# Where a segment's output rows are stored from: GpSimd at its end, or SP inside the next segment

## The chip, the cores and the metric

One Trainium2 chip, one NeuronCore of it. The metric is the device time of one execution in microseconds. Engines: TensorE (PE, its weight loads PEld), VectorE (DVE), ScalarE (ACT), GpSimd (POOL) and SyncE (SP), each with a queue of its own that it works through in order. SP and GpSimd issue DMAs here; all transfers run on the same 16 DMA engines.

## The reference

Two independent parts, whose results stand side by side in the output's columns. Part A is a dilated sliding-window attention over 2048 rows. Part B, in which the change lies, is a recurrence over 64 segments of 32 rows. Each segment puts 8 memory rows in front of its own 32, runs an attention with 32 heads of 192 over these 40 rows, and its first 8 output rows are the memory of the next segment:

```python
for s in range(n_seg):
    xs = x[:, s * seg_len:(s + 1) * seg_len, :].copy()
    h = jnp.concatenate([mem, xs], axis=1)
    q = jnp.einsum('btd,dhe->bhte', h, Wq)
    k = jnp.einsum('btd,dhe->bhte', h, Wk)
    v = jnp.einsum('btd,dhe->bhte', h, Wv)
    scores = jnp.einsum('bhqe,bhke->bhqk', q, k) * scale
    ...
    p = _softmax(scores, axis=-1)
    o = jnp.einsum('bhqk,bhke->bhqe', p, v)
    o = jnp.einsum('bhte,hed->btd', o, Wo)
    mem = o[:, :M, :].copy()
    outs.append(o[:, M:, :])
```

Here `Dm` is 640, `M` is 8 and `seg_len` is 32. The weights of part B are bfloat16, 640 x 6144 each for q, k and v and 6144 x 640 for the output, more than fits on the chip beside the rest.

## The kernel before

**Tiling.** The 32 heads go in 4 groups of 8. Of each weight matrix a group has pieces: five for q, k and v (one per 128 rows of the input, 128 x 1536, 384 KB) and six for the output (128 x 1280, 320 KB). Most pieces stay in SBUF (`wres`). The 23 of `STREAMED` do not fit: they are copied once to DRAM in a layout that reads well (`wcopy`), and each segment fetches them again: k0 has 3 streamed pieces, k1 2, k2 3, v0 1, k3 2, v1 2, the output's group 0 one (o3), v2 2, v3 3, and the output four more (o15, o16, o20, o21). "k2" is the key projection of group 2.

**Time order.** The rows of a segment are split: the memory and the first 24 rows of the segment are its `main` 32 columns; the last 8 rows of several segments are projected together ahead of time (`ahead`), and their q and k are kept in blocks (`Lb`, made by line 591, `turn_late`) until the segment that uses them, which copies them into place (line 607, `fill_late`). Every segment renews one group of k and one of v (`RENEW`: k0 and v2 in each fourth segment, and so on); then its projection works on `ahead` and `main` together, and the `ahead` half goes first to the one buffer `sb` (line 567).

**Order of the work.** `ORDER` lists the steps of a segment by name, and the program is written in that order; TensorE, VectorE, ScalarE and SP keep it, while GpSimd's order is made by a scheduler. `q`, `k`, `v` with a group are projections (line 561), `e` and `ve` empty their PSUM banks (lines 567, 600, 614, 616), `T` turns the result and fills the late columns, `S` is the scores (line 625), `sb` to `send` the softmax, `tp` and `PT` spread it, `mix` multiplies by v (line 688), `ot` keeps the result (line 696) and sends its late rows from GpSimd to DRAM (lines 697 and 698, `late_o`), `out` and `last` are the output projection (lines 713 and 739), and `close` ends the segment: it writes the next segment's memory into `HX` (line 747), the segment's 32 rows into the tile `XS` (line 748), and stores 24 of them with four DMAs from GpSimd (line 750), one for each 160 columns.

**The fetches.** A step that needs a streamed piece asks `get_unit`, which issues the fetch of it from SP (line 474) into one of seven slots (`nbuf` 7) at that place of the program. SP runs ahead of TensorE: it issues a fetch as soon as the slot's former piece is used up, that is seven fetches ahead. SP also loads the next segment's rows into `XS` (line 534, `load_x`, at step `ve.2`), after the stores have read it.

**What the change touches.** `close` (lines 743 to 751) and `step` inside `segment` (lines 766 to 831), and by them the order of SP's and GpSimd's queues around the end of a segment. Behind the stores, GpSimd has at that place the block copies of the next q group (line 591, step `Tql`) and the fill of the next segment's q0 (line 607, step `T.q0`).

Of the kernel before, what the change touches and what calls it, by code (L numbers as in the profile page):

```python
# [23 lines left out]
def part_a(ctx, tc, A_x, A_wqkv, A_wo, out, ident, emit_loads):  # L24
# [241 lines left out]
    with tc.manual_schedule(engines={mybir.EngineType.PE, mybir.EngineType.DVE, mybir.EngineType.Activation}):  # L266
        pq = ps_q.tile([128, BIG], FP32, tag="q")
        for _ in range(LEAD_IN):
            nc.tensor.matmul(pq[:, 0:8], lhsT=ident, rhs=ident[:, 0:8], start=True, stop=True)
# [35 lines left out]
EVACUATE = {"k0": "SV", "k1": "SS", "k2": "VS", "k3": "VS", "q0": "VV", "q1": "SS", "q2": "VS", "q3": "VS"}  # L305
HEADS = ("SV", "SV", "SS", "SV")
SPREAD = "SSVV"
LEAD_IN = 114
HEAD = 10

# [8 lines left out]
def part_b(ctx, tc, B_x, B_mem0, B_Wq, B_Wk, B_Wv, B_Wo, out, ident, n_seg, pre, nbuf, mid):  # L319
    nc = tc.nc  # L320
    Dm, H, Dh, M, SEG, L = 640, 32, 192, 8, 32, 40
# [3 lines left out]
    out2 = out.rearrange("b s d -> (b s) d")  # L325
# [203 lines left out]
    def turn32(dst, src):  # L529
        nc.vector.transpose(dst, src.rearrange("p (f k) -> p k f", k=5))  # L530
# [39 lines left out]
    def turn_in_place(t):  # L570
        nc.vector.transpose(t, t)  # L571

    def columns_of(m, n0, n1):
        t = KT[:] if m == "k" else QT[:, 0:12 * L].rearrange("p (f n) -> p f n", n=L)
        return t[:, :, n0:n1]
# [19 lines left out]
    def project_qk(s, m, g):  # L595
        return project32([ahead, main] if renewed(s, m, g) else [main], m, g)

    def evacuate(m, ps, copies):
        sb = to_sb(ps[0], copies[0]) if len(ps) > 1 else None
        copies[1](columns_of(m, 0, 32), ps[-1][:].rearrange("p (f n) -> p f n", n=32))  # L600
        return sb

    def fill_late(s, m, g, sb):
        if sb is not None:
            return turn_late(sb, m, g, s, s)
        b = late.pop((m, g, s))
        nc.gpsimd.tensor_copy(columns_of(m, 32, L), b[:])  # L607
        free.append(b)

    def values(s, g):  # L610
        return project32([ahead, main] if renewed(s, "v", g) else [main], "v", g)

    def keep_values(g, ps):
        S_(Vst[:], ps[-1][:])  # L614
        if len(ps) > 1:
            S_(LV[g][:], ps[0][:])

    def scores(g):
        Sps = bank()[:, 0:4 * L].rearrange("p (a n) -> p a n", n=L)
        for outer in range(2):  # L620
            for a in range(4):
                for h in range(2):
                    k0, k1, c = (0, 128, 2 * h) if outer else (64 * h, 64 * h + 64, 1)
                    f = 3 * a + c
                    nc.tensor.matmul(Sps[64 * h:64 * h + 64, a, :], lhsT=QT[k0:k1, L * f:L * f + 64], rhs=KT[k0:k1, f, :],  # L625
                                     start=(outer == 0 and a == 0), stop=(outer == 1 and a == 3),
                                     tile_position=(k0, 64 * h))
        return Sps

    def soft_begin(Sps):  # L630
        nc.vector.scalar_tensor_tensor(out=Sps, in0=Sps, scalar=scale,  # L631
                                       in1=mask[:].unsqueeze(1).to_broadcast([128, 4, L]),
                                       op0=ALU.mult, op1=ALU.add)
        return Sps

    def soft_max(t1):
        mx = small.tile([128, 4], FP32, tag="mx")
        nc.vector.tensor_reduce(out=mx[:], in_=t1[:], axis=AX.X, op=ALU.max)
        return mx

    def soft_exp(t1, mx):
        nc.vector.tensor_tensor(t1[:], t1[:], mx[:].unsqueeze(2).to_broadcast([128, 4, L]), op=ALU.subtract)  # L642
        nc.scalar.activation(t1[:], t1[:], ACTF.Exp)  # L643

    def soft_end(s, g, t1):
        sm = small.tile([128, 4], FP32, tag="mx")
        nc.vector.tensor_reduce(out=sm[:], in_=t1[:], axis=AX.X, op=ALU.add)
        nc.vector.reciprocal(sm[:], sm[:])
        put_p(s, g, t1, sm)
# [18 lines left out]
    def spread_p(g, pt):  # L668
        PT = one.tile([128, 4, 2, L], BF16, tag="PT")
        if SPREAD[g] == "S":  # L670
            for b in range(2):
# [71 lines left out]
    def close(s, Y, part, partT):  # L743
        Ysb, T = XS[:], Vst[:, 0:320].bitcast(FP32).rearrange("p (k n) -> p k n", n=SEG)
        if s + 1 < n_seg:
            turn32(T, Y)
            nc.vector.tensor_tensor(HX[:, 0, :, 0:M], T[:, :, 0:M], partT[:, :, 0:M], op=ALU.add)
        nc.vector.tensor_tensor(Ysb, Y, part, op=ALU.add)  # L748
        for j in range(4):
            nc.gpsimd.dma_start(out2[SEG * s:SEG * s + SEG - M, Dm + 160 * j:Dm + 160 * j + 160],  # L750
                                Ysb[32 * j + M:32 * j + SEG])

    def segment(s):
        last = s + 1 == n_seg
        engine = {"S": S_, "V": V_}
        got = {}

        def project(m, g):
            if m == "v":
                got["v", g] = values(s, g)  # L760
            else:
                got[m, g] = project_qk(s, m, g)
                if last and (m, g) == ("k", 3):
                    load_late((2, 3))

        def step(name, *at):
            g = int(at[0][-1]) if at else None
            if name in "qkv":
                project(name, g)
            elif name == "e":  # L770
                m = at[0][0]
                got["sb", m, g] = evacuate(m, got.pop((m, g)), [engine[c] for c in EVACUATE[at[0]]])
            elif name == "T":
                m = at[0][0]
                keep = fill_late(s, m, g, got.pop(("sb", m, g)))
                turn_in_place(columns_of(m, 0, 32))
                if m + at[0][1] == "k0" and s and keep:
                    got["keep"] = keep
                elif keep:
                    keep()  # L780
                if at[0] == "k1" and "keep" in got:
                    got.pop("keep")()
            elif name == "S":
                got["S", g] = scores(g)
            elif name == "sb":
                got["t", g] = soft_begin(got.pop(("S", g)))
            elif name == "mx":
                got["mx", g] = soft_max(got["t", g])
            elif name == "sub":
                soft_exp(got["t", g], got.pop(("mx", g)))  # L790
            elif name == "send":
                soft_end(s, g, got.pop(("t", g)))
            elif name == "tp":
                got["p", g] = turn_p(g)
            elif name == "PT":
                got["PT", g] = spread_p(g, got.pop(("p", g)))
            elif name == "ve":
                keep_values(g, got.pop(("v", g)))
                if g == 2:
                    load_x(s + 1)  # L800
                elif last and g == 1:
                    load_late((0, 1))
            elif name == "mix":
                got["mix", g] = mix(g, got.pop(("PT", g)))
            elif name == "ot":
                keep_mix(s, g, got.pop(("mix", g)), [engine[c] for c in HEADS[g]])
            elif name == "out":
                g, half = int(at[0]), int(at[1])
                if "Y" not in got:
                    got["Y"] = ps_y.tile([128, 320], FP32, tag="y", name="Y")  # L810
                project_out(got["Y"], g, range(4 * half, 4 + 2 * half))
            elif name == "part":
                got["part"] = join_begin(got["Y"])
            elif name == "join":
                join_end(got["Y"], got["part"])
                got["partT"] = None if last else turn_part(got["part"])
            elif name == "tx":
                turn_x(s + 1)
            elif name == "ql":
                got["ql"] = None if last else project32([ahead], "q", (s + 1) % 4)  # L820
            elif name == "eql":
                got["sbl"] = None if last else to_sb(got["ql"][0], S_)
            elif name == "last":
                got["Z"] = bank()[:, 0:160]
                project_last(got["Z"])
            elif name == "close":
                close(s, got["Z"], got["part"], got["partT"])
            elif name == "Tql":
                if not last:
                    gl = (s + 1) % 4  # L830
                    turn_late(got["sbl"], "q", gl, s, s + 1)()

        for token in (ORDER if s else FIRST).split():
            step(*token.split("."))
# [3 lines left out]
    def load_late(quads):  # L838
        for b in quads:
            nc.sync.dma_start(res[DEAD[b]], late_o[b].rearrange("p g i c -> p (g i c)"))  # L840
# [143 lines left out]
```

## Time and profile before

| what | value |
|---|---|
| median of 3 runs | 1889.4 us (1887.69 to 1894.31) |
| the profiled execution | 1890.7 us |
| its span, first to last instruction | 1888.9 us |
| first and last stores of a segment | 211.4 to 1824.4 us |
| SP's waits for a slot (line 474, on the projections) | 744.3 us |
| four stores on GpSimd | 2.02 us |

Part A fills the first 200 us or so, the 64 segments run from there to about 1824 us, and a projection of all late rows ends the kernel. A row of the timeline gives start, duration, engine, line, operation, what is written and read, the count, and in brackets the idle time of the engine before it with what ended it. A row of the waits gives who waited for whom, the total in us, the number of times and the longest. In the windows the columns are the stretch, its length, the busy time of PE, PEld, DVE, ACT and POOL with their instructions, the granted TensorE clock, the busy share of the DMA engines and GB/s.

### The profile page before, as it was taken

How to read it: one execution, taken by the hardware profiler on the slowest of the kernel's cores; microseconds unless marked ns; L12 is line 12 of the kernel's file. 1: busy time of each engine (PE TensorE's matmuls, PEld its weight loads, DVE VectorE, ACT ScalarE, POOL GpSimd, SP SyncE). 2: the span in 40 equal slices, each digit the busy share in tenths (PEclk: the TensorE clock that was granted, in tenths of full speed). 3: DMA queues.
4: the chain of work that ended last, by engine and by line, in shares of the span. 5: the costliest groups of instructions: out<-in, count | busy, mean ns of one | idle time of the engine just before them, and what ended most of it. 6: DMA issues, size and time to landing. Idle time of an engine off the chain costs nothing.

```text
span 1888.9 us, 91408 instructions
## 1 busy us (share of the span) xinstructions
PE 1638.2 (87%) x39286; PEld 1050.2 (56%) x39286; DVE 1239.6 (66%) x3561; ACT 720.8 (38%) x1931; POOL 689.8 (37%) x1876
## 2 busy tenths in 40 slices
PE   8898898888888989888889888888888888888887
PEld 5565555555555555555555555555555555555567
DVE  4786666766666766666667666667676666666630
ACT  4454333333343433334334334333333433333420
POOL 3001334434334444434434333444344334344321
PEclk9999999999999999999999999999999999899999
DMA  9926999999999999999999999999999999999991
GB/s 333 312 71 234 382 343 357 363 332 354 357 342 351 373 350 367 342 322 358 356 342 371 356 325 345 366 355 349 351 368 354 346 348 361 312 360 347 353 351 31
DMA packets 276849, 627.62 MB, mean 332 GB/s; under 512 B 60084, under 2 KB 75890, under 8 KB 276444
## 3 DMA queue, kind: packets, MB, share of 16 engines
q1 hardware_dynamic: 257596, 608.42, 89.7%
q0 software_dynamic: 18784, 13.32, 2.3%
q8 instruction: 308, 5.05, 1.1%
q14 instruction: 97, 0.79, 0.1%
q10 hardware_dynamic: 64, 0.04, 0.0%
HBM read 607.47 MB, written 22.91 MB: 334 GB/s over the span
## 4 chain that ended last, share of the span: by engine, by line
PE 58%; DMA 16%; DVE 9%; issue 7%; POOL 5%; ACT 4%; SPq 0%; POOLq 0%; DVEq 0%; ACTq 0%
PE acc L561 29%; DMA t<-wcopy_v 8%; PE Y L713 7%; DMA t<-wcopy_k 5%; PE px L625 4%; PE px L688 4%; PE pq L95 3%; PE px L739 3%; PE px L664 2%; POOL out_dram L750 2%; DMA late_o<-OL 2%; ACT OT L696 1%; PE px L856 1%; DVE prod L151 1%; ACT QT L720 1%
## 5 line engine op out<-in xcount | busy, mean ns | idle before, releaser
L561 PEld LDWEIGHTS <-HX 128*32 128x32 bf16 x19380 | 513.4, 97 | 412.9 <-issue 173.7
L561 PE MATMUL acc<-t,HX 128*32 128x384 bf16 x5812 | 442.5, 331 | 54.6 <-issue 19.1
L561 PE MATMUL acc<-wres_q,HX 128*32 128x384 bf16 x6460 | 328.8, 331 | 33.9 <-issue 22.6
L697 POOL COPY OL<-OT 128x96 bf16<-128x96 bf16 x256 | 158.9, 621 | 367.5 <-ACT OT L696 263.3
L561 PE MATMUL acc<-wres_v,HX 128*32 128x384 bf16 x3876 | 257.8, 331 | 16.6 <-issue 15.5
L561 PE MATMUL acc<-wres_k,HX 128*32 128x384 bf16 x3232 | 226.8, 329 | 4.7 <-issue 4.1
L600 ACT CAST QT<-acc 128x384 bf16<-128x384 f32 x192 | 93.1, 485 | 335.0 <-PE px L625 326.8
L713 PE MATMUL Y<-wres_o,OT 128*32 128x320 bf16 x3840 | 204.6, 302 | 10.4 <-issue 9.7
L696 ACT CAST OT<-px 128x240 bf16<-128x240 f32 x320 | 113.3, 358 | 241.4 <-PE px L688 237.2
L696 DVE CAST OT<-px 128x240 bf16<-128x240 f32 x192 | 78.1, 407 | 164.2 <-PE px L688 157.3
L571 DVE STREAM_TRANSPOSE QT<-QT 128x384 bf16<-128x384 bf16 x256 | 145.9, 570 | 40.6 <-ACT QT L600 40.6
L698 POOL DMA_DIRECT2D late_o<-OL x256 | 139.4, 545 | 81.5 <-POOL OL L697 72.4
L625 PE MATMUL px<-KT,QT 64*64 64x40 bf16 (+1 forms) x4096 | 139.0, 189 | 32.2 <-POOL QT L607 14.8
L625 PEld LDWEIGHTS <-QT 64*64 64x64 bf16 (+1 forms) x4096 | 108.5, 109 | 103.3 <-issue 53.2
L607 POOL COPY QT<-Lb 128x96 bf16<-128x96 bf16 x252 | 66.7, 265 | 239.2 <-PE px L625 239.2
L631 DVE SCALAR_TENSOR_TENSOR px<-px,mask 128x160 f32<-128x160 f32 x256 | 83.9, 328 | 102.7 <-PE px L625 101.7
L713 PEld LDWEIGHTS <-OT 128*32 128x32 bf16 x4608 | 115.4, 97 | 62.6 <-issue 24.5
L571 DVE STREAM_TRANSPOSE KT<-KT 128x384 bf16<-128x384 bf16 x256 | 140.6, 549 | 0.0
L750 POOL DMA_DIRECT2D out_dram<-XS x256 | 129.3, 512 | 14.6 <-DVE XS L748 7.9
L614 ACT CAST Vst<-acc 128x384 bf16<-128x384 f32 x256 | 124.2, 485 | 25.7 <-PE acc L561 24.7
L688 PE MATMUL px<-PT,Vst 64*128 64x80 bf16 (+1 forms) x2048 | 123.8, 213 | 3.8 <-issue 3.7
L643 ACT ACTIVATE px<-px 128x160 f32<-128x160 f32 x256 | 73.7, 288 | 129.4 <-DVE px L642 122.7
(103 smaller groups left out, 2434.2 us busy)
## 6 DMA issues: line engine op xcount, KB each, us to landing
t<-wcopy_k SPq DMA_DIRECT2D x640, 384.0 KB, 5.4
t<-wcopy_v SPq DMA_DIRECT2D x512, 384.0 KB, 5.9
t<-wcopy_o SPq DMA_DIRECT2D x330, 320.0 KB, 5.5
wres_q<-in_B_Wq_dram SPq DMA_DIRECT2D x20, 384.0 KB, 7.9
late_o<-OL POOLq DMA_DIRECT2D x256, 24.0 KB, 5.1
wres_q<-late_o SPq DMA_DIRECT2D x16, 384.0 KB, 7.3
wres_o<-in_B_Wo_dram SPq DMA_DIRECT2D x19, 320.0 KB, 7.3
wres_v<-in_B_Wv_dram SPq DMA_DIRECT2D x12, 384.0 KB, 7.9
```

The costliest lines, as they stand in the source:

```text
L561: nc.tensor.matmul(ps[n][32 * j:32 * j + 32].rearrange("p (f n) -> p f n", n=32), lhsT=X[:, dc, :], rhs=columns(w, (m, g, dc), j), start=( ...
L571: nc.vector.transpose(t, t)
L600: copies[1](columns_of(m, 0, 32), ps[-1][:].rearrange("p (f n) -> p f n", n=32))
L614: S_(Vst[:], ps[-1][:])
L625: nc.tensor.matmul(Sps[64 * h:64 * h + 64, a, :], lhsT=QT[k0:k1, L * f:L * f + 64], rhs=KT[k0:k1, f, :], start=(outer == 0 and a == 0), st ...
L631: nc.vector.scalar_tensor_tensor(out=Sps, in0=Sps, scalar=scale, in1=mask[:].unsqueeze(1).to_broadcast([128, 4, L]), op0=ALU.mult, op1=ALU ...
L688: nc.tensor.matmul(ps[r][lo:hi, 2 * L * k:2 * L * k + 2 * L], lhsT=V[64 * r:64 * r + 64, col:col + hi - lo], rhs=PT[64 * r:64 * r + 64, 2 ...
L696: copy(OT[:, 6 * r:6 * r + 6].rearrange("p c n -> p (c n)"), ps[r][:, 0:6 * L])
L697: nc.gpsimd.tensor_copy(OL[:, g % 2].rearrange("p n c -> p c n"), OT[:, :, 32:L])
L698: nc.gpsimd.dma_start(late_o[s // 4][:, g, s % 4], OL[:, g % 2].rearrange("p n c -> p (n c)"))
L713: nc.tensor.matmul(Y[t:t + 32].rearrange("p (b c) -> p b c", b=2), lhsT=OT[:, slot(c), 0:32], rhs=quarter(w, ("o", i, 0), 2 * r + gv), sta ...
L750: nc.gpsimd.dma_start(out2[SEG * s:SEG * s + SEG - M, Dm + 160 * j:Dm + 160 * j + 160], Ysb[32 * j + M:32 * j + SEG])
```

## The change

The four stores of a segment are no longer issued by GpSimd in `close`. `close` puts their source and target on a list, `stores`, and the next segment issues them from SP, one each ahead of the steps `T.k1`, `PT.0`, `T.k2` and `S.2` of `ORDER`. The last segment still issues its own from GpSimd.

```diff
+STORE_AT = ("T.k1", "PT.0", "T.k2", "S.2")
...
         nc.vector.tensor_tensor(Ysb, Y, part, op=ALU.add)
-        for j in range(4):
-            nc.gpsimd.dma_start(out2[SEG * s:SEG * s + SEG - M, Dm + 160 * j:Dm + 160 * j + 160],
-                                Ysb[32 * j + M:32 * j + SEG])
+        stores.extend((out2[SEG * s:SEG * s + SEG - M, Dm + 160 * j:Dm + 160 * j + 160], Ysb[32 * j + M:32 * j + SEG])
+                      for j in range(4))
+        if s + 1 == n_seg:
+            while stores:
+                nc.gpsimd.dma_start(*stores.pop(0))
+
+    stores = []
...
         def step(name, *at):
             g = int(at[0][-1]) if at else None
+            if ".".join((name,) + at) in STORE_AT and stores:
+                nc.sync.dma_start(*stores.pop(0))
```

`ORDER` itself is unchanged. Around the four places it reads

```python
T.q1 k.2 sub.0 T.k1 S.1 e.q2 send.0 e.k2 sb.1 tp.0 mx.1 T.q2 PT.0 v.0 sub.1 ve.0 T.k2 k.3 S.2
```

and since a fetch is issued at the step that asks for the piece, SP's queue gets, after the three fetches of k2: store 1, store 2, the fetch of v0, store 3, the two of k3, store 4, the two of v1, and on as before. The reload of `XS`, some fetches later, now comes behind stores of the same queue.

## Prediction

> **What bounds the kernel now.** I read the page first (busy shares, DMA queues, chain that ended last), then windows, then the waits, then the timeline of single segment boundaries, and last what SP issues.
>
> ```profile
> span 1888.9 us, 91408 instructions
> PE 1638.2 (87%) x39286; PEld 1050.2 (56%) x39286; DVE 1239.6 (66%) x3561; ACT 720.8 (38%) x1931; POOL 689.8 (37%) x1876
> q1 hardware_dynamic: 257596, 608.42, 89.7%
> PE 58%; DMA 16%; DVE 9%; issue 7%; POOL 5%; ACT 4%; SPq 0%; POOLq 0%; DVEq 0%; ACTq 0%
> ...
> 300.00:1800.00 1500.00, 1302.91 (x32629) 819.91 (x32632) 1017.12 (x3133) 579.77 (x1610) 599.98 (x1643) 0.99 0.98 351
> ...
> 1107.30:1111.30 4.00, 2.43 (x56) 1.19 (x54) 1.84 (x5) 0.58 (x2) 2.35 (x10) 1.00 1.03 391
> 1123.30:1130.50 7.20, 6.57 (x204) 4.35 (x202) 5.46 (x18) 3.42 (x10) 3.05 (x7) 1.00 0.88 300
> ```
>
> Two resources run near their ends together. In 300 to 1800 us (segments alone) TensorE is busy 1303 of 1500 us and the DMA engines have work 0.98 of the time at 351 GB/s; no granted clock is lost (0.99). Short stretches lie on both sides of that: 391 GB/s in one where TensorE stalls, 300 GB/s in one where it is busy 6.57 of 7.20 us. So neither is a hard wall: a TensorE stall that is saved must be followed by weights that come as much sooner.
>
> By the Trainium skill (DMA: Bandwidth & Descriptors, "Where 436 GB/s comes from"), HBM gives one core some 358 GB/s. By that only 2% of the segments' time, some 31 us, could be won by anything that leaves the bytes as they are. The stretch at 391 GB/s does not agree, so I do not take it as a wall.
>
> ```profile
> by line: PE acc L561 33.3%; DMA t<-wcopy_v 9.4%; PE Y L713 8.3%; issue 8.1%; DMA t<-wcopy_k 5.5%; PE px L688 4.8%; PE px L625 4.8%; PE px L739 3.2%; PE px L664 2.8%; POOL out_dram L750 2.6%; DMA late_o<-OL 2.5%; ACT OT L696 1.6%; ACT QT L72
> ...
> L750 POOL DMA_DIRECT2D out_dram<-XS x256 | 129.3, 512 | 14.6 <-DVE XS L748 7.9
> ...
> ACT sb L567 <- POOL Lb L591: 47.2, 14, 5.7
> PE px L625 <- POOL QT L607: 14.8, 16, 2.4
> PE px L625 <- POOL Lb L591: 3.7, 13, 0.5
> PE acc L561 <- ACT sb L567: 12.0, 11, 3.4
> PE acc L561 <- DMA t<-wcopy_v: 12.5, 33, 0.8
> PE acc L561 <- DMA t<-wcopy_k: 8.3, 17, 1.4
> ```
>
> The first row is the chain from 200 to 1830 us. The stores hold 2.6% of those 1630 us, 42 us, which at 2.02 us for four (next fence) is 21 boundaries of 64. The rows of waits tell what that stops on TensorE: 14.8 us until GpSimd has filled QT, 3.7 until it has done the blocks of `late`, 12.0 until ScalarE has emptied a bank, 30.5 us together. It waits 20.8 us for v and k weights beside that, in 50 places.
>
> **What the change removes.** Four issues of 512 ns leave GpSimd at the end of 63 segments, and nothing on it waits for them any more. Two kinds of boundary, in the timeline:
>
> ```profile
> 1105.99 2.02 POOL L750 DMA_DIRECT2D out_dram<-XS  x4
> 1108.01 0.88 POOL L591 COPY Lb<-sb 128x96 bf16<-128x96 bf16 x4
> 1108.92 0.48 ACT L567 CAST sb<-acc 128x384 bf16<-128x384 f32 x1 [3.99 <-POOL Lb L591]
> 1109.45 0.35 PE L561 MATMUL acc<-t,HX 128*32 128x384 bf16 x4 [0.42 <-ACT sb L567]
> 1110.62 0.54 PE L625 MATMUL px<-KT,QT 64*64 64x40 bf16 x16 [0.17 <-POOL Lb L591]
> ...
> 1076.75 2.02 POOL L750 DMA_DIRECT2D out_dram<-XS  x4
> 1079.59 0.26 POOL L607 COPY QT<-Lb 128x96 bf16<-128x96 bf16 x1
> 1079.90 0.54 PE L625 MATMUL px<-KT,QT 64*64 64x40 bf16 x16 [0.39 <-POOL QT L607]
> ...
> 1131.23 2.02 POOL L750 DMA_DIRECT2D out_dram<-XS  x4
> 1134.08 0.26 POOL L607 COPY QT<-Lb 128x96 bf16<-128x96 bf16 x1
> 1135.23 0.54 PE L625 MATMUL px<-KT,QT 64*64 64x40 bf16 x16
> ```
>
> First kind (segments that renew k0, every fourth, 15 of them): the one buffer `sb` is read by the four block copies of L591, these stand behind the stores, and ScalarE cannot write k0's `sb` before. Without the stores the copies begin at 1105.99, end near 1106.9, and k0 is emptied some 2 us sooner. ScalarE's 14 waits average 3.4 us, more than the 2.02 taken away, so the whole time of the stores is saved there, and the TensorE waits behind it, 12.0 + 3.7 = 15.7 us, are each shorter than 2 us on average (1.1 and 0.3) and nearly all go. I take 11 us: once they are gone, weights become due sooner, and about a third meets those.
>
> Second kind: the scores wait for a fill of QT behind the stores (0.39 us at 1079.90), or do not wait at all (1135.23). All 16 waits are 14.8 us. They can go, as the mean of 0.9 us is under 2.02, but the next thing that TensorE reads is the group 2 key pieces, and those already end 8.3 us of its waits. I take 3 us of the 14.8. Together 14 us; the bounds are 0 (the weights take all of it) and 30.5 (all three rows).
>
> **What it adds to SP.** Two stores behind the third streamed piece of k2, one between v0 and k3, one behind k3. SP then issues 28 DMAs a segment, not 24.
>
> ```profile
> SPq L474 <- PE acc L561: 744.3, 758, 10.6
> ...
> L474 SPq DMA_DIRECT2D t<-wcopy_k x640: 319/320/2462, 106.3 to 1797.6; - x160
> DMA to landing us min/median/max: 2.8/5.7/8.1
> ...
> L869 SPq DMA_DIRECT2D out_dram<-wres_q x18: 492/588/1537, 1852.5 to 1880.3; - x18
> ...
> 1020.01 7.57 SPq L474 DMA_DIRECT2D t<-wcopy_k  x8
> 1027.67 0.79 SPq L474 DMA_DIRECT2D t<-wcopy_v  x1
> 1028.55 0.87 SPq L474 DMA_DIRECT2D t<-wcopy_k  x2
> 1030.40 2.52 SPq L474 DMA_DIRECT2D t<-wcopy_v  x2
> ...
> 1035.14 0.32 SPq L534 DMA_DIRECT2D XS<-xwindows  x1
> ...
> t<-wcopy_k SPq DMA_DIRECT2D x640, 384.0 KB, 5.4
> out_dram<-XS POOLq DMA_DIRECT2D x256, 7.5 KB, 5.0
> ```
>
> Issue time: no store from SP stands in the segments. The nearest rows are a fetch (320 ns) and SP's own stores at the end (588 ns): 1.3 to 2.4 us a segment. I take 2.0, nearer to the stores. SP waits 744.3 us for free slots, 11.8 us a segment, which covers it; but v0 and the two k3 pieces, issued back to back here, go 1.2 to 1.8 us later.
>
> New waits: the built program gives SP's DMAs eight semaphores in turn, and one is not used again before its last DMA has landed. With seven slots and few other DMAs, that never came last. With the stores between, the first v1 piece stands eight DMAs behind the third k2 piece and must wait until that has landed; the fourth store likewise on the second k2 piece. In the segment shown the last k2 piece is issued at 1027.26 (its 0.32 us end the 7.57) and lands, by the median of 5.4, near 1032.7; v1's first went out at 1030.40. So v1's issue comes 2.3 us later, and v1's second, o3 and v2 queue behind it on SP.
>
> What that costs: three pieces (v0, k3, k3) are still in the queue then. One takes 393 KB / 351 GB/s = 1.12 us, the three 3.36 us, and the shortest time from issue to landing is 2.8 us, its own 1.12 among them, so a fetch needs 1.7 us before its bytes move. 3.36 covers 1.7 on average, with 1.7 to spare; the queue is merely shallower. Nothing is lost while it stays so. If only one piece is left ahead, 0.6 us are lost, which is the upper end (63 x 0.6 = 38 us); the lower is 0. I take 0.1 us, nearer to 0 because three pieces lie ahead: 6 us over 63 segments.
>
> The stores' bytes are the same from either queue: 30 KB a segment, 0.09 us at 351 GB/s, no term.
>
> The Trainium skill says (the same page, "Why a DMA increments its semaphore by 16 and not by 1") that a transfer of 24 rows uses 12 engines, from SP always the lowest-numbered, from GpSimd consecutive ones that move on in turn. By it an estimated 0.03 us a segment (30 KB on 12 engines against 16), 2 us in all, would come on top; no run here shows it yet.
>
> The reload of XS now waits for the fourth store, which lies in the queue right behind k3 and lands with it; the reload went out (1035.14) 5.7 us after k3 and is read at the segment's end. That costs nothing; were the store as late as 8.1 us, the v3 pieces behind the reload would be some 2 us late.
>
> **Sum.** -14 + 6 = -8 us. The profiled execution took 1890.7 us, 1.8 more than its span and 1.3 above the median of 1889.4. 1890.7 - 8 = 1882.7, against the median 1881.4; I say 1882.
>
> **Rivals.**
> 1. *The weights take it all* (no change). For it: 33 waits on v pieces and DMA busy 0.98. Then TensorE reaches the scores sooner and waits for k2 and v3: 14 falls to 4 and stands against 6, some 1890. Against it: 391 GB/s shows that the queue can go faster where it is kept full.
> 2. *The semaphores starve the queue* (slower). One mechanism: SP stands in front of v1's first piece until the last k2 piece lands, and meanwhile fetches whose slots are free are not issued. It decides when the three pieces ahead are done in less than 1.7 us plus SP's issue times, so when k2's landing is late or k3's issue, moved by 1.8 us, has thinned the queue already. At 0.35 us a segment it is 22 us, less 8 for the boundaries that still gain: 1904. For it: v pieces are the largest DMA share of the chain (9.4%). Against it: 3.36 us of work ahead.
> 3. *GpSimd's stall comes through whole* (larger gain): 30.5 of TensorE, 2 lost on SP: 1861. Against it: the k pieces are already waited for.
>
> That the change leaves the boundary as it is cannot be: the block copies follow the last late output in GpSimd's new order.
>
> **Chances.** Forecast (1872 to 1884) 0.38; no change 0.22; slower 0.31; large gain 0.09. Against the median, 0.3% is 5.7 us, about what a measurement can tell from none. Faster 0.46 (the forecast's upper end gives a little to no change), same 0.23, slower 0.31. The range of 8 in 10 is 1864 to 1906, from the large gain to past rival 2; the forecast's own is 1872 to 1884.
>
> **What would show it.** Right: GpSimd's block copies L591 start within 0.3 us of its last issue for `late_o`; ScalarE's wait on them falls from 47.2 us under 20; the three TensorE rows from 30.5 us under 8; SP has a new wait on the landing of k pieces ahead of v1, 1 to 2 us a segment; waits on v weights rise from 12.5 to at most 20 us; GB/s over 300 to 1800 rises to 353. Wrong: waits on v weights above 30 us or GB/s under 350 (rival 2); k weights waited for 15 us more with the time unchanged (rival 1); the three rows unchanged (the boundary hangs on something else).

## The result and the profile after

| | median | lowest to highest | runs |
|---|---|---|---|
| before | 1891.86 us | 1878.31 to 1909.36 | 6 |
| changed kernel | 1911.70 us | 1905.72 to 1918.85 | 6 |

The ratio is 1.012, with a 95% interval of 1.0078 to 1.0161: the change makes the kernel about 1.2% slower, some 23 us. Every ratio in this text leaves out the few executions that ran slow, so it is not the quotient of the medians given beside it. The forecast was 1882 us with a range of 1864 to 1906, so the measured median lies outside the range.

In the changed kernel every line behind `STORE_AT` is one higher: the fetch is L475, the projections L562, the block copies L592; the stores from SP are L774. The page of the changed kernel, with its span, busy times, the queue of SP's DMAs, and the chain that ended last by engine and by line:

```profile
span 1910.5 us, 91248 instructions
PE 1649.0 (86%) x39286; PEld 1052.2 (55%) x39286; DVE 1239.9 (65%) x3561; ACT 722.6 (38%) x1931; POOL 566.5 (30%) x1624
q1 hardware_dynamic: 266668, 610.37, 89.9%
PE 49%; DMA 36%; DVE 5%; issue 4%; ACT 3%; SPq 1%; POOL 0%; POOLq 0%; DVEq 0%; ACTq 0%
PE acc L562 23%; DMA t<-wcopy_v 21%; DMA t<-wcopy_k 14%; PE Y L714 7%; PE px L689 3%; PE px L740 3%; PE pq L95 3%; PE px L626 3%; PE px L665 2%; PE px L863 1%; ACT OT L697 1%; ACT QT L721 1%; DVE prod L151 1%; PE po L161 1%; PE acc L863 1%
```

SP's queue carries 9072 packets more than before. GpSimd has left the chain (5% before, 0% now), and 123 us of its busy time are gone. But the DMAs went from 16% of the chain to 36%, nearly all of it fetched v and k pieces. The waits of TensorE and ScalarE, and behind them those of SP, say the same (who waited for whom, total us, times, longest):

```profile
PE acc L562 <- DMA t<-wcopy_v: 50.1, 102, 2.4
PE acc L562 <- DMA t<-wcopy_k: 32.3, 61, 1.5
PE px L626 <- POOL Lb L592: 6.2, 12, 0.5
...
PE acc L562 <- ACT sb L568: 1.4, 2, 0.8
...
ACT sb L568 <- POOL Lb L592: 7.5, 3, 3.7
...
SPq L475 <- PE acc L562: 448.6, 586, 10.7
SPq L475 <- DMA t<-wcopy_k: 51.9, 92, 1.6
SPq L475 <- DMA t<-wcopy_v: 49.6, 101, 1.6
SPq L535 <- DMA out_dram<-XS: 46.2, 44, 2.4
SPq L774 <- DMA t<-wcopy_k: 24.7, 44, 2.3
```

Read it in two halves. The first half of the change worked: ScalarE's wait on the block copies fell from 47.2 to 7.5 us, and TensorE's wait on GpSimd's fill is no longer listed. The second half cost more than that: TensorE waits 82.4 us for v and k pieces (20.8 before), and SP, which before spent 744.3 us waiting for free slots (L474 on `acc`), waits only 448.6 us for them. Instead it stands in front of transfers that have not landed: 101.5 us ahead of fetches (24.2 before), 24.7 ahead of stores, 46.2 ahead of the reload of `XS` (0.3 before).

The stretch of segments, 300 to 1800 us, in the windows of the changed kernel (stretch, length, busy time of PE, PEld, DVE, ACT, POOL, granted clock, DMA share, GB/s):

```profile
300.00:1800.00 1500.00, 1299.40 (x32235) 812.82 (x32234) 1005.29 (x3096) 574.82 (x1591) 477.44 (x1389) 0.99 0.97 346
```

351 GB/s have become 346, with the DMA engines busy 0.97 of the time instead of 0.98. The program moves the same pieces; that 1.4% less of them goes in a microsecond agrees with the slowdown. Where in a segment it arises shows in the timeline of SP around one boundary of the changed kernel (start, duration, engine, line, operation, count; a boundary's `XS` add runs at 1033.53):

```profile
1034.81 0.32 SPq L475 DMA_DIRECT2D t<-wcopy_k  x1
1035.18 1.63 SPq L774 DMA_DIRECT2D out_dram<-XS  x2
1036.90 0.35 SPq L475 DMA_DIRECT2D t<-wcopy_v  x1
1037.30 0.39 SPq L774 DMA_DIRECT2D out_dram<-XS  x1
1037.79 0.82 SPq L475 DMA_DIRECT2D t<-wcopy_k  x2
1039.13 0.33 SPq L774 DMA_DIRECT2D out_dram<-XS  x1
1040.09 1.85 SPq L475 DMA_DIRECT2D t<-wcopy_v  x2
```

In the segment that the prediction shows, v0, the two k3 pieces and v1's first began 0.1, 1.0 and 2.8 us after the last k2 fetch ended (at 1027.58). Here v0 begins 1.8 us, k3 2.7 us and v1 5.0 us after the k2 fetch ended at 1035.13. Over 58 segments, from the trace's rows, in us after the `XS` add that ends the segment before (end of the issue, then landing):

```
piece            before           changed kernel
k2, third     1.94 ->  6.77      1.85 ->  6.46
v0            2.66 ->  7.81      3.44 ->  7.76
k3, first     3.37 ->  8.91      4.51 ->  9.41
k3, second    4.48 -> 10.10      5.23 -> 10.49
v1, first     5.32 -> 11.25      6.94 -> 11.80
v1, second    7.40 -> 12.35      7.73 -> 12.96
v2, second    9.84 -> 15.52      9.65 -> 16.35
```

Two delays are in it. v0 and k3 leave 0.75 to 1.14 us late, for the issues of the stores stand ahead of them. v1's first leaves 1.62 us late, 0.48 us after the third k2 piece has landed: that piece is the one eight DMAs ahead of it, and its semaphore is used again. In the trace of every run SP's DMAs take the same eight semaphores in turn, and no fetch or store starts before the one eight ahead of it has landed. k3's second piece is held in the same way by the first k2 piece: in half of the segments it leaves within 0.25 us of that landing. By v2 the fetches are issued on time again, yet that piece lands 0.83 us late. The time was lost in the queue in between.

### The profile page after: what moved, and what is told of

Its sections match the earlier page's. It is cut to its first block, busy times and chain, and to the rows that moved or that the text cites. A ratio compares the mean times of both kernels' runs of the same rounds, so it can differ in the third digit from the quotient of the medians.

```text
span 1910.5 us, 91248 instructions
## 1 busy us (share of the span) xinstructions
PE 1649.0 (86%) x39286; PEld 1052.2 (55%) x39286; DVE 1239.9 (65%) x3561; ACT 722.6 (38%) x1931; POOL 566.5 (30%) x1624
## 4 chain that ended last, share of the span: by engine, by line
PE 49%; DMA 36%; DVE 5%; issue 4%; ACT 3%; SPq 1%; POOL 0%; POOLq 0%; DVEq 0%; ACTq 0%
PE acc L562 23%; DMA t<-wcopy_v 21%; DMA t<-wcopy_k 14%; PE Y L714 7%; PE px L689 3%; PE px L740 3%; PE pq L95 3%; PE px L626 3%; PE px L665 2%; PE px L863 1%; ACT OT L697 1%; ACT QT L721 1%; DVE prod L151 1%; PE po L161 1%; PE acc L863 1%
## 5 line engine op out<-in xcount | busy, mean ns | idle before, releaser
L562 PEld LDWEIGHTS <-HX 128*32 128x32 bf16 x19380 | 517.3, 97 | 451.6 <-issue 211.1
L562 PE MATMUL acc<-t,HX 128*32 128x384 bf16 x5812 | 444.9, 329 | 100.8 <-DMA t<-wcopy_v 50.1
L562 PE MATMUL acc<-wres_q,HX 128*32 128x384 bf16 x6460 | 326.3, 331 | 21.7 <-issue 10.8
L562 PE MATMUL acc<-wres_v,HX 128*32 128x384 bf16 x3876 | 256.2, 330 | 8.4 <-issue 7.6
L562 PE MATMUL acc<-wres_k,HX 128*32 128x384 bf16 x3232 | 221.4, 327 | 3.9 <-issue 3.5
L601 ACT CAST KT<-acc 128x384 bf16<-128x384 f32 x192 | 92.9, 484 | 81.2 <-PE px L626 46.9
```

The source lines that it names most:

```text
L562: nc.tensor.matmul(ps[n][32 * j:32 * j + 32].rearrange("p (f n) -> p f n", n=32), lhsT=X[:, dc, :], rhs=columns(w, (m, g, dc), j), start=( ...
```

## The experiments

Each kernel is given against the kernel before, measured beside it on the same chip (medians of 6 to 12 runs against 17 to 23). Lines of kernels with a new DRAM buffer or scratch tile are a few higher again. "Waits" are TensorE's on `wcopy_v` and `wcopy_k` together at the projections: 20.8 us in the kernel before, 82.4 in the changed one. The theories: (1) SP's fetches go out late, through the issues and the semaphores of the stores; (2) the stores' transfers themselves cost it.

**e1: the change without its stores.** The rows of all segments but the last are not stored.

```diff
-                nc.sync.dma_start(*stores.pop(0))
+                stores.pop(0)
```

> The changed kernel with the stores of all segments but the last left out (their rows are not written). It tells what the free GpSimd is worth with nothing added to SP. If the gain at the boundary is real (my 14 us of the prediction) the time is about 1876; if the weights take it all it is within 5 us of before, about 1887 to 1892. The changed kernel's own loss is then its distance to this run: about 35 us or about 20.

Measured: 1880.74 us against 1892.93, ratio 0.9947 (0.9918 to 0.9977), waits 30.2 us. The stall on GpSimd was worth 0.5%, about 10 us (4 to 16 by the interval). e1 leaves out the bytes of the stores too, but e4 below stores all of them and has 0.9939. What SP does with the stores costs the distance from there to 1.012: 0.0173 x 1892 = 33 us, 0.52 us for each of 63 segments.

**e2 and e5: a tiny load in place of each store.** Four loads of 16 rows of 80 bytes (1.25 KB) go at the places of the stores, and the rows of all segments but the last are not stored. In e2 all four write the same 16 rows of a scratch tile (`scratch[0:16]`), in e5 each its own; the edit shown is that of e5.

```diff
-                nc.sync.dma_start(*stores.pop(0))
+                j = 4 - len(stores)
+                stores.pop(0)
+                nc.sync.dma_start(scratch[32 * j:32 * j + 16], XW[0, 0, 0:16, 0:40])
```

> In place of the four stores SP issues four loads of 16 x 80 bytes at the same four places (the segments' rows are not written). The issues on SP and the waits on semaphores are those of the changed kernel, but almost no bytes move and nothing is written. Theory 1 (SP's issue time and its semaphores keep the fetches back): as slow as the changed kernel, 1905 to 1915. Theory 2 (the stores' own transfers hold up the fetches in SP's queue): as fast as the kernel without stores, 1875 to 1890.

Measured in e2: 2161.79 us, ratio 1.142 (1.1368 to 1.1471), far from both theories. The waits of SP in e2 tell why:

```profile
SPq L475 <- PE acc L562: 410.1, 550, 10.8
SPq L776 <- DMA scratch<-xwindows: 406.2, 187, 6.0
```

As all four write the same rows, each waits until the one before has landed, and SP stands 406.2 us with fetches queued behind. This run doesn't separate the theories; it does show that holding SP is dear: 281 us over e1 with 406.2 us of standing. Not all of it need be the standing, since the granted TensorE clock was lower as well (0.91 from 300 to 1800 us, 0.99 in e1).

> The tiny loads again, each to rows of its own, so that none waits for the one before it. SP's issues and the waits for its eight semaphores are those of the changed kernel, nothing is stored (the segments' rows are not written) and almost no bytes move. Theory 1 (issues and semaphores keep the fetches back): 1905 to 1918 as the changed kernel. Theory 2 (the stores' transfers hold up the fetches): 1875 to 1885 as the kernel without stores.

Measured in e5: 1916.86 us, ratio 1.0122 (1.0084 to 1.0161), waits 84.1 us. With 5 KB a segment instead of 30 KB, and no store at all, the loss is that of the changed kernel. The stores' bytes and their direction aren't the cause: theory 2 falls. In e5 SP waits for no store ahead of the reload of `XS` either, so the loss does not need the 46.2 us there.

**e3: all four stores at one later place.** `S.2` lies behind the k3 fetches, so the stores no longer stand ahead of v0 and k3, but four in a row ahead of v1.

```diff
-            if ".".join((name,) + at) in STORE_AT and stores:
+            while ".".join((name,) + at) == "S.2" and stores:
```

> All four stores at S.2, behind k3's fetches and ahead of v1's: v0 and k3 are issued as in the kernel before, v1's first piece still waits for the last k2 piece, now also behind four issues in a row. Theory 1, if it is the lateness of v0 and k3: about 1895. Theory 1, if it is v1's wait: 1908 to 1918. Theory 2: unchanged, 1908 to 1915.

Measured: 1934.07 us, ratio 1.0216 (1.0171 to 1.026), above each of the times expected. Of SP's waits and TensorE's in e3:

```profile
SPq L475 <- DMA t<-wcopy_k: 114.6, 167, 3.0
SPq L475 <- DMA t<-wcopy_v: 108.4, 197, 2.5
...
PE acc L562 <- DMA t<-wcopy_v: 95.4, 152, 2.3
PE acc L562 <- DMA t<-wcopy_k: 14.7, 30, 1.7
```

The loss moved with the place: k pieces are waited for less than in the changed kernel (14.7 against 32.3 us), the v pieces behind the stores more (95.4 against 50.1). Four DMAs in a row take four of the eight semaphores, which leaves four for fetches at that place, and SP stands 223 us ahead of fetches for unlanded pieces.

**e4: one store.** One store of all 128 rows at `T.k1` to a DRAM buffer, and four copies from there to the output behind the last segment.

```diff
-        stores.extend((out2[SEG * s:SEG * s + SEG - M, Dm + 160 * j:Dm + 160 * j + 160], Ysb[32 * j + M:32 * j + SEG])
-                      for j in range(4))
+        stores.append((YD[s].rearrange("j n c -> (j n) c"), Ysb))
...
+            if first:
+                rows = out2.rearrange("(s n) d -> s n d", n=SEG)
+                for j in range(4):
+                    nc.gpsimd.dma_start(rows[:, 0:SEG - M, Dm + 160 * j:Dm + 160 * j + 160], YD[:, j, M:SEG])
```

> One store of all 128 partitions of XS (40 KB) at T.k1 to a DRAM buffer laid out like the tile, and four copies from DRAM to DRAM at the end of the kernel in place of the rest. One issue and one semaphore in place of four, a third more bytes, all 16 engines. Theory 1: a quarter of the loss, so 1880 to 1890 with some 3 us for the copies at the end. Theory 2 by bytes: as slow as the changed kernel, 1905 to 1915; theory 2 by the number of separate transfers: 1885 to 1895.

Measured: 1885.26 us against 1892.93, ratio 0.9939 (0.9903 to 0.9975), waits 33.0 us. More bytes than the change stores (40 KB against 30 KB a segment), and nothing of the loss is left.

**e6: two stores of 64 rows,** at `T.k1` and `PT.0`, so back to back ahead of v0, into the same buffer.

```diff
+        stores.extend((YD[s, 2 * h:2 * h + 2].rearrange("j n c -> (j n) c"), Ysb[64 * h:64 * h + 64]) for h in range(2))
```

> Two stores of 64 partitions each, at T.k1 and PT.0, to the DRAM buffer, with the copies at the end. One issue more ahead of v0 than with one store, but v1's first piece then stands eight DMAs behind the first k2 piece, which has long landed: the semaphores hold nothing back. Theory 1a (semaphores): as with one store, 1880 to 1890. Theory 1b (SP's issue time): a third of the way to the changed kernel, 1890 to 1897.

Measured: 1903.25 us, ratio 1.005 (1.0023 to 1.0077), waits 64.1 us: slower than either reading gave. The DMA eight ahead of v0, k3 and v1 has landed long before in this kernel (k0's last at 0.75 us for v0, which leaves at 4.08; k2's first at 4.25 for v1's first, which leaves at 5.84). So for these pieces it is mostly issue time that counts: v0 leaves 1.42 us later than in the kernel before. The kernel is not free of the semaphores for all that. SP stands for landed pieces later in the segment, most of all ahead of o3, which takes its turn eight DMAs behind the third k2 piece; of SP's waits in e6, together 67.3 us:

```profile
SPq L476 <- DMA t<-wcopy_v: 39.7, 97, 2.1
...
SPq L476 <- DMA t<-wcopy_k: 27.6, 57, 1.3
```

**e7: four stores of 32 rows** at the places of the change, into the buffer.

```diff
+        stores.extend((YD[s, j], Ysb[32 * j:32 * j + 32]) for j in range(4))
```

> Four stores of 32 partitions at the four places of the changed kernel, to the DRAM buffer, with the copies at the end. Issues, semaphores and places are the changed kernel's, but each store has 32 rows and so, by the Trainium skill's rule on 24 rows and 12 engines, spreads over 16. Theories 1a and 1b: 1905 to 1920. If the uneven 12 engines are the cause: 1880 to 1890.

Measured: 1916.30 us, ratio 1.0101 (1.0056 to 1.0146), waits 79.1 us, as the changed kernel. How many rows a store has makes no difference that can be seen.

**e8: semaphores alone.** The one store of e4, and three tiny loads (into rows of their own) ahead of the third k2 fetch, where SP waits for a slot anyway.

```diff
+            if (m, g, dc) == ("k", 2, 4) and stores:
+                for j in range(3):
+                    nc.sync.dma_start(scratch[32 * j:32 * j + 16], XW[0, 0, 0:16, 0:40])
```

> The kernel with one store, and three tiny loads in each segment right ahead of the fetch of the third k2 piece, where SP waits more than 1.5 us for a free slot anyway. They take no time from v0 and k3, but they use three semaphores: k3's second piece now waits for the second k2 piece, some 1 us longer than before. Theory 1a (semaphores): clearly slower than with one store, 1895 to 1910. Theory 1b (issue time): as with one store, 1880 to 1890.

Measured: 1915.69 us, ratio 1.0117 (1.0082 to 1.0153), waits 82.4 us: semaphores cost more than either reading gave. Of e8's timeline of SP and its waits:

```profile
1045.71 1.35 SPq L562 DMA_DIRECT2D scratch<-xwindows  x3
1047.16 1.41 SPq L476 DMA_DIRECT2D t<-wcopy_k  x1
1048.67 0.38 SPq L777 DMA_DIRECT2D ywindows<-XS  x1
1049.16 0.36 SPq L476 DMA_DIRECT2D t<-wcopy_v  x1
1050.19 1.59 SPq L476 DMA_DIRECT2D t<-wcopy_k  x2
...
SPq L476 <- DMA t<-wcopy_k: 91.2, 144, 1.5
SPq L476 <- DMA t<-wcopy_v: 44.7, 104, 1.3
```

Between the fetch of v0 (ended 1049.52) and that of k3 (1050.19) SP stands. Over 58 segments the two k3 pieces leave 4.99 and 5.98 us after the boundary; the k2 pieces eight DMAs ahead of them land at 4.30 and 5.37. So each leaves 0.6 to 0.7 us after that landing. The third k2 fetch is issued later too (2.47 us against 1.94), and v0 leaves at 3.94 us against 3.27 in e4, so e8 isn't free of issue time; but from k3 on it is the semaphore that decides.

**e9, e10: stores apart, and the last of them late.** e9 has the two stores of e6 at `T.k1` and `part`, e10 the four of the change at `T.k1`, `v.2`, `PT.3` and `part`. `PT.3` and `part` come behind the reload of `XS`, so the stores there carry rows of the next window in place of the results.

```diff
-STORE_AT = ("T.k1", "PT.0", "T.k2", "S.2")
+STORE_AT = ("T.k1", "part")
...
+STORE_AT = ("T.k1", "v.2", "PT.3", "part")
```

> The two stores of 64 rows of e6, but the second goes at the step 'part' (between the fetches of o20 and o21's neighbours, some 15 DMAs after the first and 6 after the XS load), so no run of eight DMAs of SP holds more than two small ones and only one stands ahead of the fetches of v0 and k3. Theory 'crowding' (a small DMA costs only where it shares a run of eight with others, because a fetch may not go out before the DMA eight ahead of it has landed): like one store, 1880 to 1892 us, ratio 0.994 to 1.000, the SP waits on a landed wcopy_k or wcopy_v under 45 us together (e6 had 67). Theory 'count' (every further DMA on SP costs the same wherever it goes, 0.5% for the second): like e6, 1897 to 1907 us.

> The changed kernel's own four stores of 24 rows, from SP, into the output directly, but at four places spread over the segment (T.k1, v.2, PT.3, part) instead of four within seven DMAs. Theory 'crowding': most of the loss goes, 1882 to 1896 us, ratio 0.995 to 1.002, the waits of TensorE on wcopy_v and wcopy_k under 45 us together (82 in the changed kernel). Theory 'count': the loss stays, 1908 to 1918 us, ratio 1.009 to 1.014, waits of TensorE on the weights about 80 us.

Measured in e9: 1901.50 us, ratio 1.0048 (1.0012 to 1.0083), waits 41.8 us. In e10: 1981.81 us, ratio 1.0494 (1.0447 to 1.0541). e10 answers another question than the one asked:

```profile
SPq L475 <- PE acc L562: 412.0, 512, 13.1
SPq L535 <- DMA out_dram<-XS: 223.0, 62, 5.0
```

Its `v.2` store is issued three DMAs ahead of the reload of `XS`, which must wait for it to land, and SP stands 3.6 us in every segment. In e9 the theory "crowding" is half right: the waits of SP on landed pieces are 34.9 us, under the 45 expected, but the time is that of "count".

```profile
SPq L773 <- DMA XS<-xwindows: 21.1, 28, 2.3
SPq L476 <- DMA t<-wcopy_v: 18.2, 48, 1.1
SPq L476 <- DMA t<-wcopy_k: 16.7, 38, 1.2
```

So sharing a run of eight isn't all that costs. Its second store stands ahead of o20, which leaves 0.9 us later than before (7.86 us ahead of the boundary against 8.77); and the store itself holds SP 21.1 us in all until `XS` has landed. How much each of these two bears is open. The place of the loss fits, though: from 18 to 22 us after the boundary, where o20 and o21 are issued, the DMA engines moved 328 and 305 GB/s (in 2 us each; 347 and 328 before).

**e11: one store from GpSimd.** The store of 128 rows of e4 goes from GpSimd at the segment's end; SP's queue is that of the kernel before.

```diff
+        stores.append((YD[s].rearrange("j n c -> (j n) c"), Ysb))
+        nc.gpsimd.dma_start(*stores.pop(0))
```

> One store of 128 rows to a DRAM buffer from GpSimd at the segment's end, four copies from there to the output at the kernel's end; SP issues what it did before the change. If the stall of the copies at the start of a segment is worth 10 us for four stores, one store leaves about a quarter of the wait behind: 1880 to 1887 us, ratio 0.993 to 0.997, the ScalarE wait on the L593 copies 10 to 25 us (47.2 before). If the gain of e4 came from elsewhere (the order of the stores' transfers), 1889 to 1895 us.

Measured: 1880.23 us against 1891.81, ratio 0.9945 (0.9915 to 0.9974). Of e11's groups, waits and windows:

```profile
L752 POOL DMA_DIRECT2D ywindows<-XS x64 | 34.5, 538 | 9.5 <-issue 3.9 <-DVE QT L573 2.8 <-DVE XS L750 2.6
...
ACT sb L569 <- POOL Lb L593: 23.2, 9, 3.7
PE acc L563 <- DMA t<-wcopy_k: 17.5, 36, 2.0
PE acc L563 <- DMA t<-wcopy_v: 11.2, 28, 0.9
...
300.00:1800.00 1500.00, 1321.14 (x33154) 833.87 (x33154) 1025.75 (x3170) 587.71 (x1631) 521.47 (x1485) 0.99 0.99 358
```

One issue of 538 ns instead of four of 512 leaves half of ScalarE's wait (23.2 of 47.2 us) and gains the same as no store at all. e4 and e11 beat both kernels, the one before by some 0.6%, their four copies at the end included; their intervals overlap, so neither is shown to be the better one.

**e12: the same two stores as e6, one of them in SP's gap.** The first goes ahead of the third k2 fetch, where SP waits some 2 us for a slot, the second at `T.k1`.

```diff
+            if (m, g, dc) == ("k", 2, 4) and stores:
+                nc.sync.dma_start(*stores.pop(0))
```

> The two stores of 64 rows of e6, but the first goes ahead of the third k2 fetch, in the 2 us in which SP waits for a slot anyway, and only the second stands at T.k1 ahead of v0. No fetch from v0 on has more issue time of SP ahead of it than in e4, and none has to wait for a landed piece that is late. Theory 'late fetches' (what costs is that the fetches of v0, k3 and v1 go out later, and fewer than four pieces are in flight then): like e4, 1880 to 1892 us, ratio 0.994 to 1.000, TensorE's waits on wcopy_v and wcopy_k under 45 us together. Theory 'count' (each DMA on SP beyond the first costs the same wherever it goes): like e6 and e9, 1897 to 1907 us, ratio 1.003 to 1.008.

Measured: 1889.96 us against 1894.06, ratio 0.9997 (0.9965 to 1.0029), and TensorE's waits in e12:

```profile
PE acc L565 <- DMA t<-wcopy_v: 20.3, 45, 1.4
PE acc L565 <- DMA t<-wcopy_k: 17.0, 43, 1.2
```

37.3 us, under the 45 of "late fetches", and the time inside its range, at the upper end. The same two stores cost less when SP has time for one of them (1.005 in e6, though the two intervals just touch): "count" alone doesn't hold. The expectation has it that no fetch must wait for a late landing; that did not come true:

```profile
SPq L476 <- DMA t<-wcopy_k: 37.6, 65, 2.5
...
SPq L476 <- DMA t<-wcopy_v: 28.3, 64, 1.3
```

With 65.9 us SP stands here as long as in e6 (67.3), without e6's loss. So it is not SP's standing in sum that prices a store, but which fetch leaves later, and by how much: v0 leaves at 3.51 us here, at 4.06 in e6.

**All of them on one scale.** Worked out from the traces: how many streamed pieces are on their way (issued, not landed) when v0, the two k3 pieces and v1's first are issued, mean of the four over the segments between 300 and 1800 us; and what the DMA engines moved from 4 to 12 us after the boundary, mean over 56 segments. Both come from the one profiled execution, whose time stands beside them; it can lie 1% off the kernel's median (e11's is the fastest of its twelve).

```
kernel                        pieces   GB/s   profiled us   ratio
e11 one store, GpSimd          4.47    369    1861.0        0.9945
e1  no stores                  4.39    360    1888.9        0.9947
before                         4.28    357    1890.7        1
e4  one store, SP              4.16    355    1877.2        0.9939
e12 two stores, one in gap     3.88    345    1881.5        0.9997
e6  two stores ahead of v0     3.43    329    1892.4        1.0050
changed kernel                 3.26    320    1912.3        1.012
e8  one store, 3 tiny loads    3.07    320    1926.2        1.0117
e5  4 tiny loads               3.07    306    1913.9        1.0122
e7  4 stores of 32 rows        3.06    308    1921.6        1.0101

stores (also) at other places:
e10 four apart                 4.37    362    1977.7        1.0494
e9  two apart                  4.19    350    1904.3        1.0048
e3  four ahead of v1           3.96    325    1934.9        1.0216
```

In the upper part, with fewer than four pieces on their way less is moved there, and the kernel is slower; above four the order is lost (e4 has fewer than the kernel before and is faster, but "before" has the stall on GpSimd beside that). What it takes to thin the queue, mostly issue time (e6), semaphores (e8 from k3 on) or both (the change), makes no difference that this table shows. The scale reads one place of the segment and is none for the lower part: e9 and e10 lose their time later in the segment, and e3 from v1's first on, of which the mean holds only one piece in four (2.93 are on their way then). e2, which stands still for each load, is left out.

## Why the prediction was wrong, point by point

**What bounds the kernel: right.** TensorE and the DMA engines both run near their ends, and what the change gained for the one was lost at the other.

**What the change removes: right.** 14 us (0 to 30.5) were predicted, e1 shows 10 (4 to 16). The three rows of TensorE waits, 30.5 us, were to fall under 8; they are 6.2 on the block copies and 1.4 on ScalarE, 7.6 us. ScalarE's wait was to fall under 20 us and is 7.5. At the boundary at 1033.53 the block copies start 0.4 us behind GpSimd's last `late_o` issue, not 0.3, since a fill of `KT` now goes ahead of them:

```profile
1034.39 0.54 POOL L699 DMA_DIRECT2D late_o<-OL  x1 [0.29 <-POOL OL L698]
1034.92 0.28 POOL L608 COPY KT<-Lb 128x96 bf16<-128x96 bf16 x1
1035.34 0.89 POOL L592 COPY Lb<-sb 128x96 bf16<-128x96 bf16 x4
```

**What it adds to SP, the delays: right in kind, too large in size.** A store from SP was taken at 500 ns (2.0 us for four); the rows of L774 in the changed kernel (minimum, median, maximum in ns) have 392:

```profile
L774 SPq DMA_DIRECT2D out_dram<-XS x252: 306/392/1407, 212.3 to 1819.7; - x126
```

v0 and k3 were to go 1.2 to 1.8 us later (measured 0.75 to 1.14), v1's first 2.3 us later, held by the landing of the third k2 piece (measured 1.62, 0.48 us behind that landing). So the loss is not that of longer delays: shorter ones than predicted cost more than five times the predicted 6 us.

**What the delays cost: wrong, and this is the step that failed.** "3.36 covers 1.7 on average, with 1.7 to spare; the queue is merely shallower. Nothing is lost while it stays so. If only one piece is left ahead, 0.6 us are lost"; from this came 0.1 us a segment, 6 us. Measured: 0.52 us a segment, 33 us. The count of pieces was right (2.98 are on their way when v1's first is issued, 4.61 before), and so was a piece's 1.12 us (the landings before stand 1.04 to 1.19 us apart from the third k2 to v1's second piece). What was wrong is that three pieces on their way move as much as four or five. From 4 to 12 us after the boundary, the DMA engines moved 320 GB/s in place of 357: 8 x (357 - 320) / 357 = 0.83 us of transfers put off. Part of it is made up: from 14 to 20 us after the boundary the changed kernel moves 373 to 384 GB/s (347 to 364 before). A queue doesn't work at full rate down to its last piece and then stop.

The traces also say in which respect three pieces were too few. Each piece has 16 completions in the trace, and in the kernel before they are spread over 2.1 us on the mean, from first to last. "Landed" is the last of them, so a piece still counted as on its way can be done in most of its parts. Counted by the first completion, there were not 3.36 us of work ahead. When v0, k3's first and v1's first had been issued in the changed kernel, the first completion of the piece ahead was only 1.07, 1.48 and 1.40 us off (before 2.00, 2.42 and 2.70): less than the 1.7 us that the prediction itself asked for. Accordingly the first completions of v0 and of v1's first come 1.50 and 1.37 us behind those of the pieces ahead of them (1.12 and 1.09 before), and from 4 to 12 us the DMA engines are busy 0.94 of the time instead of 0.98. The likely reading is that some of the engines ran dry while others were still behind. It is argued from these counts and not shown: the completions don't tell the engines apart, no run changed their spread, and 1.7 us isn't a sharp bound (e4 has 1.45 us at v0 and loses nothing that shows).

**The choice between the bounds** went wrong with it: 0 to 38 us was right as a range, 0.1 us a segment was taken as nearer to 0 for a reason that no row carried, while the row of the v pieces in the chain (9.4% before) spoke against it.

**The bytes and the XS reload: right.** e5 has a sixth of the bytes and the same time. SP's wait ahead of the reload, expected to cost nothing, came (46.2 us), but e5 has none on a store there and is as slow.

**The Trainium skill's 12 engines for 24 rows** (DMA: Bandwidth & Descriptors, "Why a DMA increments its semaphore by 16 and not by 1") were worth an estimated 2 us. e7 stores 32 rows at a time and has 1.0101 (1.0056 to 1.0146) beside 1.012: no run here shows a difference in time, and 2 us are below what this can show. The counts of packets agree with the 12 engines: SP's queue carries 9072 more for 252 stores, 36 each, which is 24 rows and 12 completions; in e7 it carries 12096 more, 48 each, 32 rows and 16.

**The rivals.** Rival 2, "the semaphores starve the queue", is what happened, with its signs (v waits above 30 us: 50.1; GB/s under 350: 346). Its price was 0.35 us a segment, too low, and it lacked a part: e6 shows that the issues of the stores thin the queue ahead of v0, k3 and v1 as well, where the semaphores hold little back. Its point of decision, three pieces done in less than 1.7 us, isn't how the loss sets in, as long as a piece is taken to be there until its last part has landed. Rival 1 (no change) and rival 3 (1861) didn't come.

**The Trainium skill's 358 GB/s of HBM** (DMA: Bandwidth & Descriptors, "Where 436 GB/s comes from") would have left 2% to win. That section of the Trainium skill halves a stack's 716 GB/s between two cores; here one core ran. e11's profiled execution, the fastest of its twelve, has just 358 in its row of the windows; but its own means from 6 to 12 us after the boundary are 374 to 378, and between 300 and 1800 us TensorE still has pauses. So no run here shows it as a wall for short stretches, and none passes it over 1500 us.

## What to carry to other kernels

When an engine's queue feeds a stage that runs near the DMA limit, price everything put on that queue by how many transfers are on their way afterwards, not by whether the engine has idle time in sum: 744 us of idle time didn't cover 99 us of issues (252 stores of 392 ns), since the idle time lay elsewhere. Count the semaphores too: where DMAs take eight in turn, each small one takes a place from the fetches around it, whatever its size. The cheap repairs were fewer, larger DMAs (one store in place of four) and places at which the queue's engine waits anyway.

## What the runs showed of the hardware that wasn't expected

- A DMA's size didn't matter here, the number of DMAs and their place did: four loads of 1.25 KB (e5) cost as much as four stores of 7.5 KB or 10 KB (1.0122, 1.012, 1.0101), while one store of 40 KB cost nothing that shows (0.9939 against 0.9947 without any).
- With about three 384 KB pieces on their way the engines moved some 306 to 320 GB/s, with 4.3 to 4.5 some 357 to 369. Busy shares over 300 to 1800 us hardly show it (0.97 and 0.98 in the changed kernel and before); in the stretch itself they do (0.94 and 0.98).
- The 16 completions of one 384 KB piece were spread over 2.1 us on the mean in the kernel before, nearly twice the 1.12 us that a piece takes when they follow each other.
- A store's issue time on SP doesn't follow its size. The rows of the stores of 64 rows (e6) and of 128 rows (e4; minimum, median, maximum in ns) beside the 392 of the stores of 24 rows:

```profile
L773 SPq DMA_DIRECT2D ywindows<-XS x126: 451/588/1538, 210.9 to 1802.0; - x126
```

```profile
L773 SPq DMA_DIRECT2D ywindows<-XS x63: 423/432/1622, 213.4 to 1785.6; - x63
```

Two of the first kind in a row are 1.18 us at the median, which is most of the 1.42 us by which v0 leaves later in e6.
